# A transformer block's opening: modulation by slices of 128 channels, later vectors on GpSimd and ScalarE

## The chip, the cores and the metric

The kernel runs on one core of one Trainium2 chip. The metric is the device time of one execution in microseconds (us), lower is better. TensorE (PE) does matrix products, VectorE (DVE), ScalarE (ACT) and GpSimd (POOL) do elementwise work, and SyncE (SP) issues most DMA transfers. Each engine takes its instructions in one order that is fixed when the program is built, so an instruction that waits holds everything behind it on its engine.

## The reference

A block with two halves, each scaled and shifted by vectors made from a conditioning row `c`. S = 2048 positions, D = 512 channels, 32 heads of 16, window 256, F = 1792.

```python
mod = (_silu(c) @ w_mod).reshape(c.shape[0], 6, 1, -1)
sa, ca, ga, sb, cb, gb = (mod[:, 0], mod[:, 1], mod[:, 2], mod[:, 3], mod[:, 4], mod[:, 5])
h = _layernorm(x, axis=-1) * (1 + ca) + sa
x = x + ga * _A_ref(h, A_wqkv, A_wo)         # windowed attention
h = _layernorm(x, axis=-1) * (1 + cb) + sb
x = x + gb * _B_ref(h, B_w1, B_w3, B_w2)     # gated feed-forward
```

The six vectors of `mod` have 512 numbers each; the first two (`sa`, `ca`) are needed before the first product of the attention, the others much later.

## The kernel before

Activations stand with channels on the partitions: `hT` holds the normalised and modulated x, transposed, in four slices `k` of 128 channels. Every float32 operand of the large products is split in a high part in fp32r and the remainder, so each large product is three matmuls over 512 columns (high by high, high by low, low by high).

The program has a beginning and then units. The beginning works on four blocks `b` of 512 positions. Per block: four tiles `xt` of x are loaded (`load_x`); DVE takes mean and variance (`bn_stats`, `bn_aggr`); GpSimd raises the variance to -0.5 (`rstd_of`); DVE applies both (`ln_apply`, L456, four instructions); PE transposes 16 tiles of 128x128, four for each slice k (L737); ACT multiplies and adds the modulation (L463, from `modc`); DVE rounds to the high part (L465) and subtracts (L466). From `hT` PE then makes the values, 12 matmuls for each of 16 tiles (`values`, L759; ACT moves the result to `vS`, L763), and the queries and keys of units 0 to 2 (`unit_a`, 12 matmuls each, L548); the rows of these go by SP to `ringq` and `ringk` (L567, L569). The first two units' maximum scores (`unit_b`, L595 on PE, L604 on DVE) also lie in the beginning. The units proper start with L855.

`modulation(j, s, t0, at)` makes one vector of `mod`. Four chunks of `w_mod` (256 KB each) are loaded to a slot of `stage`, which is memory of `vS` that is not yet in use. PE multiplies them by silu(c) repeated 32 times (`row`, L678: four matmuls of 512 columns, each to 32 rows of the result), ACT copies the result (`out`, L684), PE adds the four parts and turns them to a column with products by a column of 1/32 (`turn`, L692, one output column each, or L689 for the two gate vectors, which stay rows), and DVE or ACT writes the result (`end`). Vectors 0 and 1 come first, 3, 4, 2 and 5 between the products of the values.

The order of the beginning is that of the numbers in the table `W`: each operation is put in a list with a time by `at(t, fn)`, and the list is sorted. The units have such a list of their own, from the table `X`, and a second schedule block; memory of the beginning (`p0`) is given back between the two (`pre.close()`).

Of the kernel before, what the change touches and what calls it, by code (L numbers as in the profile page):

```python
# [17 lines left out]
H, DH = 32, 16  # L18
# [31 lines left out]
W = dict(m=0.18, s=0.307, a=0.29, t=0.562, p=0.366, vs=1.748, vo=0.433, wq=(-1.444, 1.47, 1.587), wv0=-2.239, wvh=(-0.578, -0.445, -0.399, -0.345), wvl=(-0.193, -0.326, -0.374, -0.317), wp=1, A0=2.112, h0=0.452, h=6.002, hb=6.868, ls=3.035, la=0.875, rf=(-1.1, -0.393, 6.445), v=2, vt=1.562, mr=(-1.837, 1.507), mm=(3.653, 5.841, 7.356, 7.655), ml=(-1.346, 1.651, 2.536, 6.904), A=1.465, At=7.897, B=10.563)  # L50
# [3 lines left out]
XB = 6  # L54
# [238 lines left out]

ENGS = (
# [117 lines left out]
def block_kernel(ctx: ExitStack, tc: tile.TileContext, x, wqk, wv, wo, w13, w2, c, wmod, out):  # L412
# [9 lines left out]
    o32 = cst.tile([P, 32], F32, name="o32")  # L422
    nc.gpsimd.memset(o32, 1.0 / 32)
    modc = cst.tile([P, 4, KC], F32, name="modc")
    sc32 = cst.tile([P, KC, 32], F32, name="sc32")
# [15 lines left out]

    def rstd_of(pool, mv, n, tag):
        var = pool.tile([P, n], F32, name=tag + "v")
        nc.vector.tensor_scalar_add(var, mv[:, :n, 1], EPS)
        rs = pool.tile([P, n], F32, name=tag + "r")
        nc.gpsimd.tensor_tensor(out=rs, in0=var, in1=nhalf[:, :n], op=ALU.pow)
        return rs

    def ln_tile(pool, xin, mv, i):
        st = pool.tile([P, nc.vector.BN_STATS_DIM], F32, name="bst", bufs=4)  # L450
        nc.vector.bn_stats(st, xin)
        nc.vector.bn_aggr(mv[:, i], st)

    def ln_apply(pool, xin, mv, rs, i, tag):
        xn = pool.tile([P, D], F32, name=tag, bufs=4) if tag else xin
        nc.vector.tensor_scalar(xn, xin, mv[:, i, 0:1], rs[:, i:i + 1], op0=ALU.subtract,  # L456
                                op1=ALU.mult)
        return xn

    def mod_split(pool, hT, src, k, lo, at):  # L460

        h = pool.tile([P, BT], F32, name="h32", bufs=3)
        nc.scalar.activation(h, src, AF.Identity, bias=modc[:, at, k:k + 1],  # L463
                             scale=modc[:, at + 1, k:k + 1])
        nc.vector.tensor_copy(hT[:, 0, k, lo:lo + BT], h)  # L465
        nc.vector.tensor_tensor(out=hT[:, 1, k, lo:lo + BT], in0=h,  # L466
                                in1=hT.bitcast(F32)[:, 0, k, lo:lo + BT], op=ALU.subtract)

# [169 lines left out]

    xt = {}

    def load_x(t):
        xt[t] = p0.tile([P, D], F32, name="xt", bufs=XB)
        nc.sync.dma_start(xt[t], x[t * P:(t + 1) * P, :])


    stage = vS.rearrange("p t h d -> p (t h d)")[:, 4 * H * (DH + 1):12 * KC * P + 4 * H * (DH + 1)]
    stage = stage.rearrange("p (s k c) -> p s k c", s=3, k=KC)

    def load_mod(j, s, eng):
        for k in range(KC):  # L650
            eng.dma_start(stage[:, s, k], wmod[j, :, k])

    for t in range(2):
        load_x(t)
    load_mod(0, 2, nc.scalar)
    for t in range(2, 4):
        load_x(t)
    load_mod(1, 1, nc.sync)
    sc = cst.tile([P, KC], F32, name="sc")
    cst.tile([P, 24], F32, name="gap")  # L660
    nc.scalar.activation(sc, c_sb, AF.Silu)

    def fill_sc():
        nc.vector.tensor_copy(sc32, sc[:, :, None].to_broadcast([P, KC, 32]))

    def modulation(j, s, t0, at):

        v = {}

        def bank(n):  # L670
            v[n] = psA.tile([P, BT], F32, name="mx", bufs=MXB)
            return v[n]

        def row():

            ps = bank(0)
            for k in range(KC):
# [3 lines left out]
        def out():  # L681
            v["e"] = p0.tile([P, D], F32, name="h32", bufs=3)
            for n in range(2):
                nc.scalar.activation(v["e"][:, n * 256:n * 256 + 256], v[0][:, n * 256:n * 256 + 256], AF.Copy)  # L684

        def turn():
            ps = bank(1)
            if j in (2, 5):
                nc.tensor.matmul(ps[:32], o32, v["e"], start=True, stop=True)  # L689
                return  # L690
            for n in range(KC):
# [3 lines left out]
        def end():  # L695
            if j in (2, 5):
                r = p0.tile([P, D], F32, name="h32", bufs=3)
                nc.scalar.activation(r[:1], v[1][:1], AF.Copy)
                nc.sync.dma_start(g_dr[j // 5:j // 5 + 1, :], r[:1, :])
            else:  # L700
# [19 lines left out]
    def ln1(b, ts, ta, th, at):  # L720
        v = {}

        def stats(i):
            if i == 0:
                v["mv"] = p0.tile([P, 4, 2], F32, name="mv", bufs=2)
# [984 lines left out]
```

## Time and profile before

| | |
|---|---|
| time, median of 3 runs | 919.44 us (918.0 to 920.11) |
| the profiled execution: time | 918.07 us |
| its span, first to last instruction | 916.3 us |
| busy share of PE, DVE, POOL, ACT | 98%, 71%, 61%, 56% |

All positions in time below count from the start of the span of the profiled execution. "<-" in a row means that what stands left is written from what stands right; "[0.52 <-DVE modc L701]" means 0.52 us of idle time before the instruction, ended by that instruction of DVE. An instruction of PE has a duration with its way through the array in it; what a product costs in a row of products is the distance of the starts.

### The profile page before, as it was taken

To read this page: it belongs to the slowest core of one execution; us is meant where nothing else is said; L and a number is where in the kernel's file an instruction comes from. 1 tells how busy PE (TensorE), PEld (TensorE's weight loads), DVE (VectorE), ACT (ScalarE), POOL (GpSimd) and SP (SyncE) were. 2 spreads that over 40 slices of the span, in tenths; PEclk is the share of its full clock that TensorE was granted. 3 is DMA by queue.
4 is the path that set the end of the run, shared out by engine and by line. 5 is a ranking of instruction groups with operands and counts; after the bars stand their busy time and mean duration, and the time that the engine had idled before them with its cause. 6 is when DMAs were issued, how large, how long until landed. Compare 5 with 4: busy or idle time off the path is not lost.

```text
span 916.3 us, 18353 instructions
## 1 busy us (share of the span) xinstructions
PE 893.5 (98%) x6052; PEld 726.0 (79%) x6052; DVE 654.8 (71%) x1786; ACT 513.6 (56%) x962; POOL 555.2 (61%) x796
## 2 busy tenths in 40 slices
PE   6999999999999999989998999999999999999998
PEld 2688788888888888866776888888888888888886
DVE  7676778788887778786679668758568665565555
ACT  3433777778778777766597834343465334332330
POOL 6211687787888787867676356886569355435220
PEclk9999999999999999998999999999999999999999
DMA  9631456566655655567875677574272423231102
GB/s 330 201 93 36 109 158 171 165 173 171 178 161 165 174 159 156 144 170 220 266 224 184 211 245 247 174 235 145 85 264 65 159 76 104 66 100 43 46 24 93
DMA packets 126083, 141.73 MB, mean 155 GB/s; under 512 B 61090, under 2 KB 73890, under 8 KB 125988
## 3 DMA queue, kind: packets, MB, share of 16 engines
q1 hardware_dynamic: 125268, 139.51, 50.4%
q10 hardware_dynamic: 720, 1.05, 0.4%
q8 instruction: 48, 0.79, 0.4%
q14 instruction: 47, 0.39, 0.1%
HBM read 85.72 MB, written 34.61 MB: 131 GB/s over the span
## 4 chain that ended last, share of the span: by engine, by line
PE 85%; DMA 4%; DVE 4%; ACT 2%; POOL 2%; issue 2%; SPq 0%; ACTq 0%; POOLq 0%; DVEq 0%
PE st L1472 11%; PE mx L1472 10%; PE pj L548 9%; PE st L855 8%; PE po L905 8%; PE mx L595 7%; PE mx L1568 7%; PE st L1568 6%; PE st L759 5%; PE pj L1472 4%; PE po L1472 3%; PE po L1568 2%; PE pj L1568 2%; DMA vS<-in_wmod 1%; POOL pt L865 1%
## 5 line engine op out<-in xcount | busy, mean ns | idle before, releaser
L604 DVE CUSTOM_DVE_ANT_0 junk<-mx,mskq 128x320 bf16<-128x320 f32 (+4 forms) x512 | 216.5, 466 | 55.0 <-PE mx L595 53.0
L865 POOL TENSOR_SCALAR_AFFINE_SELECT pt<-pt 128x256 f32<-128x256 f32 x472 | 184.7, 413 | 65.9 <-ACT pt L892 26.4
L595 PE MATMUL mx<-ringk,ringq 96*128 96x320 f32 (+4 forms) x512 | 149.3, 314 | 1.6 <-DMA ringq<-qk 1.6
L548 PE MATMUL pj<-hT,wq 128*128 128x512 f32 x384 | 140.2, 401 | 0.0
L892 ACT ACTIVATE pt<-st 128x512 f32<-128x512 f32 (+1 forms) x216 | 117.3, 573 | 33.1 <-DVE st L882 27.6
L855 PE MATMUL st<-ringq,ringk 98*128 98x256 f32 (+1 forms) x536 | 128.4, 328 | 3.3 <-DMA ringq<-mT 1.9
L1067 POOL TENSOR_TENSOR w<-w,w 128x512 fp32r<-128x512 f32 (+2 forms) x49 | 85.2, 1754 | 55.9 <-ACT w L1066 55.2
L595 PEld LDWEIGHTS mx<-ringk,ringq 96*128 96x128 f32 x512 | 95.9, 190 | 13.5 <-issue 2.4
L855 PEld LDWEIGHTS st<-ringq,ringk 98*128 98x128 f32 x536 | 88.3, 191 | 13.3 <-issue 2.5
L905 PE MATMUL po<-pt,vS 128*17 128x128 f32 (+1 forms) x2144 | 89.0, 314 | 0.4 <-ACT pt L876 0.4
L548 PEld LDWEIGHTS pj<-hT,wq 128*128 128x128 f32 x384 | 71.6, 190 | 10.3
L905 PEld LDWEIGHTS po<-pt,vS 128*17 128x17 f32 x2144 | 60.8, 98 | 23.1 <-issue 5.1
L882 DVE COPY_PREDICATED st<-later,st 128x256 f32<-128x256 uint8 x152 | 62.0, 426 | 23.3 <-PE st L855 21.3
L1519 POOL TENSOR_TENSOR t<-t,t 128x512 f32<-128x512 f32 x25 | 33.5, 1342 | 65.4 <-DVE t L1507 65.4
L1472 PE MATMUL st<-b,w 128*128 128x512 f32 x270 | 67.0, 390 | 0.2 <-DVE x1a L1573 0.2
L1472 PEld LDWEIGHTS st<-b,w 128*128 128x128 f32 x270 | 50.5, 188 | 11.5 <-DVE x1a L1573 0.7
L876 ACT ACTIVATE pt<-pt 128x512 f32<-128x512 f32 (+1 forms) x96 | 52.6, 587 | 9.6 <-POOL pt L865 9.4
L860 ACT ACTIVATE pt<-st 128x512 f32<-128x512 f32 (+1 forms) x96 | 52.0, 546 | 8.8 <-PE st L855 8.1
L561 POOL TENSOR_TENSOR qk<-qkr,qk 128x512 fp32r<-128x512 f32 x32 | 41.5, 1298 | 20.0 <-ACT qk L557 19.8
L1066 ACT ACTIVATE w<-w 128x512 fp32r<-128x512 f32 (+2 forms) x56 | 42.4, 784 | 18.7 <-DMA w<-wraw 11.4
L1507 DVE TENSOR_TENSOR t<-mx,t 128x512 f32<-128x512 f32 x44 | 30.1, 685 | 29.4 <-ACT t L1514 12.5
L1507 DVE TENSOR_TENSOR t<-st,t 128x512 f32<-128x512 f32 x40 | 27.4, 686 | 26.7 <-ACT g L1495 9.3
(310 smaller groups left out, 1887.0 us busy)
## 6 DMA issues: line engine op xcount, KB each, us to landing
ringq<-qk SPq DMA_DIRECT2D x192, 64.0 KB, 2.1
ringk<-qk SPq DMA_DIRECT2D x96, 128.0 KB, 2.4
o_dr<-os SPq DMA_DIRECT2D x32, 256.0 KB, 2.2
w<-wsum SPq DMA_DIRECT2D x14, 512.0 KB, 4.3
w<-w2g SPq DMA_DIRECT2D x14, 512.0 KB, 3.7
jb<-in_w SPq DMA_DIRECT2D x24, 256.0 KB, 3.7
w<-wraw SPq DMA_DIRECT2D x14, 384.0 KB, 5.7
vS<-in_wmod SPq DMA_DIRECT2D x20, 256.0 KB, 5.0
```

The source lines that it names most:

```text
L548: nc.tensor.matmul(v["ps"], WQ[g][w][:, n // 3], hTp(i, n // 3, b * BT, BT), start=(n == 0), stop=(n == 3 * KC - 1))
L595: nc.tensor.matmul(v[i][:, :n], both_queries(a, gs), keys(NS, a, (gs + 1) * HP - n, n), start=True, stop=True)
L604: nc.vector.tensor_tensor_reduce(out=junk[:, :n], in0=v[i][:, :n], in1=mskq[:, WK - n:], scale=1.0, scalar=-3e38, op0=ALU.add, op1=ALU.max ...
L855: nc.tensor.matmul(piece(v[a, k], a, k, m), keys(NM, a, kb * P, P), queries(a, 4 * b + q, n), start=new, stop=not new or len(here(a, k)) = ...
L865: nc.gpsimd.affine_select(out=out, in_=in_, **w)
L882: nc.vector.copy_predicated(o, later, block(v[a, fk], a, fk, m))
L892: nc.scalar.activation(o, i, AF.Exp, scale=SCALE)
L905: nc.tensor.matmul(po[32 * i:32 * i + DH + 1, q * P:(q + n) * P], vS[:, 4 * b + j, 4 * g + i], piece(pt_of(a, k), a, k, m)[:, h], start=i ...
L1067: either(lambda e: e.tensor_tensor(out=lo(), in0=src(), in1=hi().bitcast(F32), op=ALU.subtract), 0.85, 0.06 + 0.0024 * n, key, kl + kh, kl ...
L1472: nc.tensor.matmul(ps(bk), WT[s, n][w][:, col], BB[t, k][r], start=start and c == 0, stop=stop and c == 5, skip_group_check=True)
L1507: return nc.vector.tensor_add(o, x, y)
L1568: nc.tensor.matmul(ps(bk), tiles[hk + (h,)][:, i * P:(i + 1) * P], w2_of(last, y, f), start=(m == 0), stop=(m == 5))
```

## The change

The two vectors needed first are made by slices of 128 channels: `mod_first(k, n)` loads the 512 KB of `w_mod` that make slice k of both vectors, and PE makes them with eight matmuls of one output column each, with the chunk of `w_mod` as the weights, so the result is a column at once; DVE adds (0, 1) and writes `modc` for slice k. The other four vectors are made without PE: `mod_later(i, n)` loads a row block of the transposed `w_mod` (256 KB, 16 of them through a ring of six slots), GpSimd multiplies it by silu(c) in every row, and ACT adds along the row with its accumulator. One transpose on PE turns the gate vectors to rows (`mod_end`). ACT loads `c` once more as a row for all 128 partitions (`crow`, 256 KB). `warm(i)` gives PE 24 products that nobody reads, from the identity in fp32r, the first 16 on half of the rows each. The order of the beginning is a list of 590 numbers (`ORDER0`); `BANK0` and `ENG0` say which PSUM pool and which of DVE and GpSimd an operation takes. Beginning and units are emitted in one schedule block.

```diff
-    def modulation(j, s, t0, at):
...
-        def row():
-
-            ps = bank(0)
-            for k in range(KC):
-                nc.tensor.matmul(ps[32 * k:32 * k + 32, :], sc32[:, k], stage[:, s, k], start=True,
-                                 stop=True)
...
-                nc.tensor.matmul(ps[:, n:n + 1], v["e"][:, n * P:(n + 1) * P], o32[:, 0:1],
-                                 start=True, stop=True)
...
+    sc_row = a1.tile([P, D], F32, name="qk2", bufs=1)
+    nc.scalar.dma_start(sc_row, crow.to_broadcast([P, D]))
+    sc = cst.tile([P, KC], F32, name="sc")
+    nc.scalar.activation(sc, c_sb, AF.Silu)
+    nc.scalar.activation(sc_row, sc_row, AF.Silu)
...
+    def mod_first(k, n):
+        if n == 0:
+            nc.sync.dma_start(raw_mod[:, k], wmod01[k])
+        elif n == 1:
+            v["mod", k] = bank(("mod", k), "mx")
+            for j in range(2):
+                for q in range(KC):
+                    nc.tensor.matmul(v["mod", k][:, j:j + 1], raw_mod[:, k, j, q], sc[:, q:q + 1],
+                                     start=(q == 0), stop=(q == KC - 1), skip_group_check=True)
+        else:
+            nc.vector.tensor_tensor(out=modc[:, 0:2, k], in0=v["mod", k][:, :2], in1=one, op=ALU.add)
...
+    def mod_later(i, n):
+        (m, k), s = divmod(i, KC), i % LATE
+        j = LATER[m]
+        if n == 0:
+            nc.sync.dma_start(ring[:, s], wmodT[m, k])
+        elif n == 1:
+            nc.gpsimd.tensor_tensor(out=ring[:, s], in0=ring[:, s], in1=sc_row, op=ALU.mult)
+        else:
+            to = gcol[:, i:i + 1] if m < 2 else modc[:, j - 1, k:k + 1]
+            nc.scalar.activation(ring[:, s], ring[:, s], AF.Copy, accum_out=to)
...
+    identr = a1.tile([P, BT], F32R, name="qk1", bufs=1)[:, :P]
+    nc.scalar.activation(identr, ident, AF.Copy)
+
+    def warm(i):
+        if i == 0:
+            v["warm"] = psA.tile([P, BT], F32, name="pj", bufs=1)
+        if i < 16:
+            n, rows, to = 2 if i >= 8 else 4, slice(HP * (i % 2), HP * (i % 2) + HP), po if i % 2 else v["warm"]
+        else:
+            n, rows, to = 4 if i < 20 else 1, slice(0, P), po
+        nc.tensor.matmul(to.rearrange("p (n c) -> p n c", n=4)[:, :n], identr[rows],
+                         identr[rows, None, :].to_broadcast([rows.stop - rows.start, n, P]), start=True, stop=True,
+                         skip_group_check=True)
...
     with tc.manual_schedule():
-        for fn in first + order:
+        for fn in begin + [units_open] + following(first) + order:
             fn()
```

Three places of the order. First PE from the first products of the program on. Before, from the last transposes of block 0 to the first products of the values (L737 transposes, L678 a modulation row, L759 and L548 products); the brackets name what an instruction waits for, with a lane of the DMA queues as DMAHW:

```order
L737 MATMUL st<-ident,xt 128x128 [waits Activation_49]
L737 MATMUL st<-ident,xt 128x128 x3
L678 MATMUL mx<-vS,sc_70 32x512 [waits DMAHW5_49,DVE_49]
L678 MATMUL mx<-vS,sc_70 32x512 [waits DMAHW6_49]
L678 MATMUL mx<-vS,sc_70 32x512 [waits DMAHW7_49]
L678 MATMUL mx<-vS,sc_70 32x512 [waits DMAHW0_49]
L759 MATMUL st<-wvh,hT 128x512 [waits DVE_49,Activation_49]
```

And of the changed kernel, first from the end of the throwaway products (L773) to the first transposes (L780), with two slices of the modulation (L709) between:

```order
L773 MATMUL po<-qk_138 128x512 x4
L773 MATMUL po<-qk_138 128x128 x4
L709 MATMUL st<-sc,vS 128x1 x16
L780 MATMUL st<-ident,xt_167 128x128
L780 MATMUL st<-ident,xt_180 128x128
```

Then, after the transposes of channel slices 0 and 1, from the third slice of the modulation to the fourth (L571 and L798 are products):

```order
L709 MATMUL mx<-sc,vS 128x1 x8
L780 MATMUL mx<-ident,xt_167 128x128
L780 MATMUL mx<-ident,xt_180 128x128
L780 MATMUL mx<-ident,xt_171 128x128
L780 MATMUL mx<-ident,xt_169 128x128
L571 MATMUL pj<-hT,wq_268 128x512
L798 MATMUL st<-wvh,hT 128x512 x3
L709 MATMUL mx<-sc,vS 128x1 x8
```

Before, all transposes of block 0 and a third modulation row stood ahead of the first product; now 24 throwaway products and two slices of the modulation stand ahead of the transposes, the third slice between those of channel slices 1 and 2, and four products ahead of the fourth, behind which come the transposes of channel slice 3.

Second DVE, around the four instructions that apply the normalisation of block 0. Before (L456 applies, L701 writes `modc`, L718 makes the low part of `wv`, L465 and L466 write `hT`):

```order
L444 TENSOR_SCALAR rs0v<-mv 128x4 [waits DVE_49]
L456 TENSOR_SCALAR xt<-xt,mv,rs0r 128x512 [waits Pool_49]
L456 TENSOR_SCALAR xt<-xt,mv,rs0r 128x512 x3
L701 TENSOR_SCALAR modc<-mx 128x4 [waits PE_49]
L718 TENSOR_TENSOR wvl<-vS,wvh 128x512 [waits DMAHW7_49,Activation_49]
L701 TENSOR_SCALAR modc<-mx 128x4 [waits PE_49]
```

Changed (L760 applies, L712 writes one slice of `modc`, L788 and L791 write `hT`, L560 the low part of the first query and key weights):

```order
L753 TENSOR_SCALAR va_195<-mv_182 128x4 [waits DVE_49]
L760 TENSOR_SCALAR xt_171<-xt_171,mv_182,rs_233 128x512 [waits Pool_49]
L712 TENSOR_TENSOR modc<-st,one 128x2 [waits PE_49]
L760 TENSOR_SCALAR xt_169<-xt_169,mv_182,rs_233 128x512
L760 TENSOR_SCALAR xt_167<-xt_167,mv_182,rs_233 128x512
L760 TENSOR_SCALAR xt_180<-xt_180,mv_182,rs_233 128x512
L712 TENSOR_TENSOR modc<-st,one 128x2 [waits PE_49]
L788 CAST hT<-h_266 128x512 [waits Activation_49]
L791 TENSOR_TENSOR hT<-h_266,hT 128x512 [waits DVE_49]
L560 TENSOR_TENSOR wq_274<-wqr,wq_268 128x512 [waits DMAHW2_49,Activation_49]
L712 TENSOR_TENSOR modc<-mx,one 128x2 [waits PE_49]
```

The write of the first slice, which waits for PE, now stands ahead of the second, third and fourth of the applying instructions. A few rows on, DVE stands like this, with the write of the fourth slice ahead of the low part of channel slice 1:

```order
L788 CAST hT<-h_270 128x512 [waits Activation_49]
L712 TENSOR_TENSOR modc<-mx,one 128x2 [waits PE_49]
L791 TENSOR_TENSOR hT<-h_270,hT 128x512 [waits DVE_49]
L788 CAST hT<-h_302 128x512 [waits Activation_49]
L791 TENSOR_TENSOR hT<-h_302,hT 128x512 [waits DVE_49]
L788 CAST hT<-h_304 128x512 [waits Activation_49]
L747 BN_STATS bst_313<-xt_205 128x6 [waits DMAHW5_49]
```

Third SP, where the rows of unit 0 are sent (L590, L592 to `ringk` and `ringq`). In the changed kernel loads for the later vectors (L720) stand between them, some of which wait for ACT to have read their slot:

```order
L592 DMA ringq<-qk_392 16x16x64 [waits DMAHW4_49,Activation_49]
L720 DMA vS<-in_wmodT 128x512 [waits DMAHW5_49,Activation_49]
L592 DMA ringq<-qk_392 16x16x64 [waits DMAHW6_49]
L590 DMA ringk<-qk_392 32x2x512 [waits DMAHW7_49]
L592 DMA ringq<-qk_392 16x16x64 [waits DMAHW0_49]
L592 DMA ringq<-qk_414 16x16x64 [waits DMAHW1_49,Pool_49]
L720 DMA vS<-in_wmodT 128x512 [waits DMAHW2_49,Activation_49]
```

Before, SP had there the loads of x of a later block and two stores of gate vectors among the same rows.

## Rows read from the trace of the kernel before

**Rows 1.** The page: busy time, share of the span and instructions of each engine.
```profile
PE 893.5 (98%) x6052; PEld 726.0 (79%) x6052; DVE 654.8 (71%) x1786; ACT 513.6 (56%) x962; POOL 555.2 (61%) x796
```

**Rows 2.** Busy by stage: us, PE, PEld, DVE, ACT, POOL, granted clock, DMA share, GB/s.
```profile
0.00:21.36 21.36, 12.67 (x57) 5.25 (x57) 16.15 (x26) 8.29 (x15) 14.21 (x27) 1.00 0.92 325
21.36:49.71 28.35, 28.35 (x144) 19.38 (x143) 17.02 (x33) 10.68 (x21) 6.41 (x6) 1.00 0.64 205
49.71:94.29 44.58, 44.58 (x222) 36.62 (x221) 30.71 (x102) 16.83 (x27) 6.34 (x5) 1.00 0.21 53
```

**Rows 3.** Timeline of the first 21.5 us: start, length, engine, line, operation, count.
```profile
1.23 2.55 ACTq L651 DMA_DIRECT2D vS<-in_wmod  x4
...
5.12 0.67 DVE L451 BATCH_NORM_STATS2 bst<-xt 128x6 f32<-128x512 f32 x1
...
10.16 1.03 POOL L446 TENSOR_TENSOR rs0r<-rs0v,nhalf 128x4 f32<-128x4 f32 x1 [3.06 <-DVE rs0v L444]
...
11.23 4.66 DVE L456 TENSOR_SCALAR xt<-xt,mv,rs0r 128x512 f32<-128x512 f32 x4 [1.15 <-POOL rs0r L446]
...
13.09 1.95 PE L692 MATMUL mx<-o,h 128*128 128x1 f32 x16
...
15.94 1.20 PE L737 MATMUL st<-ident,xt 128*128 128x128 f32 x9 [0.52 <-DVE modc L701]
...
18.82 0.41 DVE L465 CAST hT<-h 128x512 fp32r<-128x512 f32 x1
...
19.76 1.67 PE L678 MATMUL mx<-vS,sc 128*32 128x512 f32 x4 [0.30 <-DMA vS<-in_wmod]
...
21.36 0.50 PE L759 MATMUL st<-wvh,hT 128*128 128x512 f32 x1
```

**Rows 4.** Timeline of PE at the first and last modulation step among the products.
```profile
25.81 0.61 PE L759 MATMUL st<-wvh,hT 128*128 128x512 f32 x2
...
27.08 0.49 PE L759 MATMUL st<-wvl,hT 128*128 128x512 f32 x1
...
42.82 0.39 PE L759 MATMUL st<-wvh,hT 128*128 128x512 f32 x1
...
44.12 0.50 PE L759 MATMUL st<-wvl,hT 128*128 128x512 f32 x1
```

**Rows 5.** Line L678 in two stretches: durations in ns, least/median/most.
```profile
L678 PE MATMUL mx<-vS,sc x16: 592/1059/1062, 7.5 to 12.6; 128*32 128x512 f32 x16
...
L678 PE MATMUL mx<-vS,sc x8: 592/605/617, 18.1 to 20.8; 128*32 128x512 f32 x8
```

**Rows 6.** DMA: GB/s in 40 slices of 0 to 30 us; median us to landing.
```profile
GB/s 0 0 29 256 246 169 295 374 399 407 407 404 399 404 393 336 336 407 404 401 398 395 375 350 298 380 396 402 401 402 382 391 371 371 410 404 399 347 98 25
...
vS<-in_wmod ACTq DMA_DIRECT2D x4, 256.0 KB, 6.6
...
xt<-in_x SPq DMA_DIRECT2D x1, 256.0 KB, 2.9
```

**Rows 7.** Groups of POOL, ACT and DVE in the beginning: count, busy, mean ns.
```profile
L561 POOL TENSOR_TENSOR qk<-qkr,qk 128x512 fp32r<-128x512 f32 x5 | 6.8, 1367 | 19.8 <-ACT qk L557 19.8
...
L763 ACT ACTIVATE vS<-st 128x512 f32<-128x512 f32 x16 | 9.6, 597 | 24.6 <-PE st L759 24.6
...
L466 DVE TENSOR_TENSOR hT<-h,hT 128x512 fp32r<-128x512 f32 x16 | 11.1, 692 | 0.6
```

**Rows 8.** Timeline: a cast on DVE beside a busy POOL, another beside an idle one.
```profile
60.27 1.29 POOL L561 TENSOR_TENSOR qk<-qkr,qk 128x512 fp32r<-128x512 f32 x1 [1.07 <-ACT qk L557]
...
60.88 0.97 DVE L465 CAST hT<-h 128x512 fp32r<-128x512 f32 x1
...
62.49 0.42 DVE L465 CAST hT<-h 128x512 fp32r<-128x512 f32 x1
```

**Rows 9.** SP sends rows of unit 0: its timeline; the page, median to landing.
```profile
37.47 1.41 SPq L569 DMA_DIRECT2D ringq<-qk  x2
...
ringq<-qk SPq DMA_DIRECT2D x192, 64.0 KB, 2.1
```

More of the change, by code (lines that the diff above doesn't have):

```diff
@@ L411, in block_kernel @@
 @with_exitstack
-def block_kernel(ctx: ExitStack, tc: tile.TileContext, x, wqk, wv, wo, w13, w2, c, wmod, out):
+def block_kernel(ctx: ExitStack, tc: tile.TileContext, x, wqk, wv, wo, w13, w2, c, crow, wmod01, wmodT, out):
     nc = tc.nc
@@ L773, in block_kernel @@
+    ring = stage[:, stage.shape[1] - LATE * D:].rearrange("p (s c) -> p s c", s=LATE)
     ops = []
@@ new lines, in turn, with modulated, high @@
+    def turn(b, k):
+        v["t", b, k] = bank(("t", b, k), "mx")
+        for i in range(4):
+            nc.tensor.transpose(v["t", b, k][:, i * P:(i + 1) * P], xt[4 * b + i][:, k * P:(k + 1) * P], ident)
+    def modulated(b, k):
+        v["h", b, k] = p0.tile([P, BT], F32, name=f"h32{k % 2}")
+        nc.scalar.activation(v["h", b, k], v["t", b, k], AF.Identity, bias=modc[:, 0, k:k + 1],
+                             scale=modc[:, 1, k:k + 1])
+    def high(b, k):
+        nc.vector.tensor_copy(hT[:, 0, k, b * BT:b * BT + BT], v["h", b, k])
@@ new lines, in low, with value, value_out @@
+    def low(e, b, k):
+        e.tensor_tensor(out=hT[:, 1, k, b * BT:b * BT + BT], in0=v["h", b, k],
+                        in1=hT.bitcast(F32)[:, 0, k, b * BT:b * BT + BT], op=ALU.subtract)
+    def value(t, k, m):
+        if k == 0 and m == 0:
+            v["v", t] = bank(("v", t), "mx" if t == 3 else "st")
+        w, i = ((0, wvh), (0, wvl), (1, wvh))[m]
+        nc.tensor.matmul(v["v", t], hTp(w, k, t * P, P), i[:, k], start=(k + m == 0), stop=(k == KC - 1 and m == 2))
+    def value_out(t):
+        nc.scalar.activation(vS[:, t, :, :DH], v["v", t].rearrange("p (h d) -> p h d", d=DH), AF.Copy)
@@ L810, in block_kernel, with units_open @@
     for u in range(2):
-        unit_b(u, h0 + W["B"] + W["At"] * u, at, Y)
-    with tc.manual_schedule():
-        for _, _, fn, _ in sorted(ops, key=lambda o: o[:2]):
-            fn()
-    pre.close()
-    a2 = att.enter_context(tc.tile_pool(name="a2", bufs=1, reuse_waits="tile"))
+        unit_b(u, (30, 55)[u], at, y)
+    ops.sort(key=lambda o: o[:2])
+    begin = arranged([o[2] for o in ops], ops)
+    late = {}
+    def units_open():
+        pre.close()
+        late["a2"] = att.enter_context(tc.tile_pool(name="a2", bufs=1, reuse_waits="tile"))
@@ L949, in job_tile @@
     def job_tile(n):
-        jb[n] = a2.tile([P, D], F32, name=f"jb{n % 2}", bufs=1)
+        jb[n] = late["a2"].tile([P, D], F32, name=f"jb{n % 2}", bufs=1)
         return jb[n]
```

280 lines of the change are left out of this document (128 added, 152 removed), and 33 rows, old and new, of tables (BANK0, ORDER0).

## The prediction

> **What bounds the kernel now.** I read the page first. TensorE is busy for 98% of the span [rows 1], so time is won by taking work from TensorE, or where it stands still. By stage [rows 2], from the first product at 21.36 us to the first unit at 94.29 TensorE has work throughout (28.35 of 28.35 us, then 44.58 of 44.58), while VectorE has 47.7, ScalarE 27.5 and GpSimd 12.8 us of work in the same 72.9. Ahead of 21.36 TensorE works for only 12.67 us; there it waits for data. Behind 94.29 the order is the same in both kernels, and I let it take the same time.
>
> How it waits in the first stage is in the timeline [rows 3]: VectorE starts the statistics at 5.12, GpSimd gives the power at 11.19, VectorE needs 4.66 us to apply it, to 15.89, and the transposes go on behind that. The first product would have had its data at 19.23, when the first cast ended, but a modulation row stood ahead of it on TensorE, whose third chunk landed only for 19.76; so 21.36.
>
> **The sum, part by part.**
>
> *Modulation among the products, removed.* Seven pieces stand there: three rows (L678) and four turns (L692, L689). At 25.81 two products begin; at their distance of 0.23 us the next could start at 26.27, and it starts at 27.08: 0.81. The last piece: product at 42.82, next possible 43.05, in fact 44.12: 1.07. Read in this way the seven cost 0.81, 1.09, 0.81, 1.17, 1.20, 1.15 and 1.07 ([rows 4] has the first and the last of them); sum 7.3. Back comes one transpose for the gate vectors, 0.1.
>
> *The front.* ScalarE's queue carries 256 KB (`crow`) in place of 1 MB, so the x tiles land sooner: they and `crow` are 1.3 MB, which by the rates in slices of 0.75 us had been moved by 7.5 us [rows 6]. VectorE cannot start before about 5.1, since its instruction ahead is unchanged. Before, the four statistics with their aggregation and two waits for x lasted until GpSimd's start at 10.16; with earlier landings (0.67 and some 0.2 each, an estimate) they end by 9.2, and with a short step and GpSimd's 1.03 us the first applying instruction starts at 10.45, in place of 11.23 [rows 3]. It takes 4.66/4 = 1.17, to 11.6.
>
> There the new wait stands: VectorE's next instruction writes slice 0 of `modc` and holds the other three until TensorE has made that slice. TensorE makes it behind 24 throwaway products, and these wait for the identity that ScalarE copies behind silu of `crow`. `crow` is issued at 1.23; a transfer of 256 KB took 2.9 us for the first x tile and 6.6 in the median of the ScalarE queue, so it lands between 4.1 and 7.8 [rows 3, 6]; I take 5.2, since only 256 KB stand on that queue. ScalarE adds 0.6 and 0.3: the throwaways start near 6.2. They stream 8,704 columns; at 0.23 us for 512 that is 3.9 us. If the products on half of the rows run in pairs it is 2.5; no row shows such pairs. And the same modulation product took 1.059 us in the first stretch of work and 0.605 later [rows 5], 1.75 times, so 6.8 is the other end. I take 4.7, near the middle, to 10.9. The column that names the granted clock reads 1.00, which is 2.4 GHz, in both stretches [rows 2]; it does not show what the durations show.
>
> The Trainium skill ("TensorE: Matmul & The Clock Gate", "Part 1: The HAM clock gate") says that half rate is TensorE's default state and that activity releases it. By it the throwaways are paid in a pause and the products behind them are fast; the durations agree that the start is slow, and before the change the modulation rows had done that warming already.
>
> Eight matmuls of one column with their weights: sixteen passes took 1.95 us (L692) [rows 3]. So slice 0 is done at 12.85, its write at 13.1, against 11.6 where VectorE could have gone on: 1.5 us of hold. Applying ends at 16.9 (10.45 + 4.66 + two writes + 1.5), before at 15.89. Then TensorE in its new order: transposes of slices 0 and 1 (0.5 each, by the 0.12 us distance of the nine) to 17.95, modulation slice 2 to 19.9, transposes to 20.4, four products to 21.3, modulation slice 3 to 23.25, transposes to 23.75. Before, four products and all transposes were done at 21.36 + 4 x 0.23 = 22.3. The front loses **1.5 us**. With no hold it loses nothing (22.25); with `crow` at 7.8 and 6.8 us of throwaways the hold, and the loss, is 6.1.
>
> *The feed of block 0 and of block 1.* The fourth slice's write holds VectorE until 23.4, and ahead of the last low part it then has three low parts (0.69), two casts (0.42), four statistics (some 0.85 with their aggregation) and the low part of a `wv` chunk (0.69 like the others) [rows 7, 8]: 7.0 us, with the start of each some 7.5. TensorE has 33 products before it needs it, 7.5 us from 23.75; then eleven more until the transposes of block 1, which need one more power (1.03) and four applying instructions (0.5 each with GpSimd idle). That fits but for some tenths. With GpSimd busy it does not: a cast took 0.97 us beside a GpSimd instruction and 0.42 soon after [rows 8], and the four applying instructions of block 0, with GpSimd busy, 4.66. I take **1.0 us** of stall, bounds 0 and 4.
>
> The Trainium skill ("SBUF — State Buffer", "Who interferes with whom") says that VectorE's cast or two-operand work and GpSimd's work take turns at one pair of ports, each blocking the other for a whole instruction. The two casts agree. By that rule in full, with each of 24 casts and applying instructions of blocks 1 to 3 doubled, VectorE would get 0.55 x 24 = 13 us more; it has 25 us of idle time there, so this too would be a matter of single waits.
>
> *The later vectors.* Sixteen GpSimd multiplies at 1.37 us (nearest row: L561) are 21.9 us on an engine that idles for 60 of 72.9; sixteen ScalarE passes at 0.60 (L763) are 9.6 on one that idles for 45 [rows 2, 7]. Their results are needed only long after the first unit. GpSimd and ScalarE hide them: 0. If their place in line is wrong, they hold what stands behind: bounds 0 to 3, put with the rival below. On SP, unit 0's last query product ends near 31.5, ScalarE and GpSimd need 1.2 + 1.4, and nine rows with three loads between, at 0.7 us each, are out by about 41 and landed by 43 [rows 9]; TensorE comes to the first score at about 45, so the loads between cost nothing.
>
> *One block with the units:* no pause at 94.29 to be won; 0.
>
> Sum: -7.3 + 0.1 + 1.5 + 1.0 = **-4.7 us**: span 916.3 to 911.6, its time 918.07 to 913.4. The median of the runs shown lies 1.4 above that execution: **914.7 us**. The bounds give -7.8 to +3 and more.
>
> **The rivals.**
> *VectorE held by the first slice* for 4 to 6 us: `crow` lands late or the throwaways run one by one at the slow rate. For it: three engines in a row ahead of one wait. Against: TensorE has no other work there, and only 256 KB stand on that queue. The front loses 4.5 to 6: 917.7 to 919.2. The change would then do on the later vectors what it says and give it back in front.
> *The feed is what bounds*, so that the products only wait where modulation stood before: 3 to 5 us of stall in blocks 0 and 1 or behind slots of the ring: 916.7 to 919. Against: VectorE idled for 25 us there.
> *Slower: the slow rate in block 0.* Ahead of the products TensorE has only one-column matmuls, transposes and pauses for some 10 us. If the products then start at half rate, at 0.46 in place of 0.23 us, the gain is gone after 4.7/0.23 = 20 products, and after 29 of block 0's 60 the kernel is slower by over 0.2%; with all 60 it is 914.7 + 13.8 = 928. Against: before the change five microseconds of the same (one-column products, transposes, a pause of 0.5) lay between 13.09 and 18, and the modulation product at 18.1 ran in 0.605, not 1.059 [rows 3, 5].
>
> **Chances.** 0.2%, some 1.8 us, is about what a measurement of this kernel tells from no change. The forecast (911.5 to 917.5) 0.58; better than that (no hold, no stall) 0.05; VectorE held 0.15, half of it within 0.2%; the feed 0.12, two thirds of it faster; the slow rate, or a stall that I don't see, 0.10. Faster 0.58 + 0.05 + 0.07 + 0.08 = 0.78, of which I take off 0.05 for the runs' own spread of 2 us: 0.73; within 0.2% 0.15; slower 0.12. Range 910.5 to 920: it leaves out half of the best case and the slow rate.
>
> **What would show it.** First product at about 20.4 with four together and a second start at 23.8; the first score near 45 (49.71 before); the first unit's score at 89.6 (94.29). VectorE's second applying instruction starts about 1.5 us after the first ended, released by TensorE. Throwaways from 6.2 to 10.9. Sixteen L722 at about 1.4 us. The forecast fails if the first unit starts later than 92.5, and the way to it tells why: the hold in front, waits of TensorE for VectorE or GpSimd between 24 and 45, or products at a distance of 0.46.

## The result, and the profile after

The changed kernel takes 930.48 us (median of four runs: 928.0 to 930.6 in three, and 2255.8 in one that counts in no ratio), the kernel before 918.72 beside it: ratio 1.0118, interval 1.0091 to 1.0145. It is slower by 1.2%; 914.7 had been forecast. The profiled execution took 930.57 us, with a span of 928.8.

The page, busy time by engine; beside [rows 1]:
```profile
PE 903.7 (97%) x6057; PEld 736.3 (79%) x6057; DVE 658.5 (71%) x1780; ACT 519.1 (56%) x983; POOL 583.8 (63%) x819
```
Five more instructions on TensorE, and 10.2 us more of busy time. Busy time by stretch, columns as in [rows 2], with the boundaries where the same events fall now: up to steady products (the first product behind the last transposes of block 0; four products stand ahead of it), to the first score, to the first unit, and from the first product of the feed-forward part to the end:
```profile
0.00:27.09 27.09, 19.49 (x109) 17.95 (x109) 13.25 (x24) 5.69 (x9) 14.34 (x29) 0.81 0.59 214
27.09:47.25 20.16, 20.16 (x97) 16.26 (x96) 16.85 (x31) 11.59 (x24) 13.53 (x10) 1.00 0.69 202
47.25:98.01 50.76, 46.64 (x223) 36.81 (x222) 37.56 (x101) 22.81 (x51) 28.35 (x22) 1.00 0.32 94
...
489.70:928.80 439.10, 433.11 (x1881) 349.64 (x1879) 284.47 (x396) 183.38 (x295) 223.61 (x164) 1.00 0.41 133
```
And that last part in the kernel before, the same view:
```profile
485.90:916.30 430.40, 424.15 (x1881) 349.59 (x1879) 284.03 (x396) 183.01 (x296) 224.70 (x164) 1.00 0.42 135
```

| stretch | before, us | after, us | difference | forecast |
|---|---|---|---|---|
| start to steady products (before: 21.36 and four products) | 22.30 | 27.09 | +4.8 | +1.5 |
| to the first score (49.71; 47.25) | 27.41 | 20.16 | -7.25 | -7.3 + 0.1, with part of the 1.0 of the feed |
| to the first unit (94.29; 98.01) | 44.58 | 50.76 | +6.2 | rest of the 1.0 |
| to the feed-forward part | 391.6 | 391.7 | +0.1 | 0 |
| to the end | 430.4 | 439.1 | +8.7 | 0 |

So there are three losses, in three stages, against one gain of the size forecast. The largest stands where not one instruction was changed: the same 1,881 matmuls, at a granted clock of 1.00 in both, keep TensorE busy 433.11 us in place of 424.15, 4.8 ns more for each. By tiles (groups of that part from 560 to 900 us: count, busy us, mean ns), after:
```profile
L1527 PE MATMUL st<-b,w 128*128 128x512 f32 x222 | 55.3, 391 | 0.0
...
L1527 PE MATMUL mx<-b,wo 128*128 128x512 f32 x108 | 27.8, 395 | 0.0
```
The same groups before:
```profile
L1472 PE MATMUL st<-b,w 128*128 128x512 f32 x216 | 53.5, 390 | 0.0
...
L1472 PE MATMUL mx<-b,wo 128*128 128x512 f32 x108 | 27.1, 389 | 0.0
```
`b` and `w` both lie at the low end of SBUF; `wo`, like `o`, `wq` and `qk`, lies in the pools with `side="right"`, at the high end. Products with one operand from each end are the slow ones: their starts are some 233 ns apart there in place of 226.7, those of products with both operands at the low end 229. (SBUF is the memory on the chip; pools are set up from its low end, those with `side="right"` from its high end.) What the change does to the low end is to alter the small constants: `o32`, `sc32` and the unused tile `gap` go, `one` and `gcol` come. With sizes rounded up to 32 bytes they are 736 bytes now and were 1,408, so each later tile of the low end starts 672 bytes lower; the high end's stay.

The front, in the timeline (after):
```profile
6.72 0.63 ACT L665 ACTIVATE qk<-qk 128x512 f32<-128x512 f32 x1 [2.71 <-DMA qk<-in_crow]
...
7.60 0.79 PE L773 MATMUL pj<-qk 64*128 64x512 f32 x1 [7.60 <-ACT qk L764]
7.61 0.79 PE L773 MATMUL po<-qk 64*128 64x512 f32 x1
...
11.29 2.93 DVE L760 TENSOR_SCALAR xt<-xt,mv,rs 128x512 f32<-128x512 f32 x1 [1.14 <-POOL rs L756]
...
12.41 4.53 PE L709 MATMUL st<-sc,vS 128*128 128x1 f32 x32
...
14.34 0.16 DVE L712 TENSOR_TENSOR modc<-st,one 128x2 f32<-128x2 f32 x1
14.42 2.83 DVE L760 TENSOR_SCALAR xt<-xt,mv,rs 128x512 f32<-128x512 f32 x3
...
18.85 3.41 PE L709 MATMUL mx<-sc,vS 128*128 128x1 f32 x16
...
22.87 0.78 PE L571 MATMUL pj<-hT,wq 128*128 128x512 f32 x1
```
The throwaways (the 24 products that nobody reads) last from 7.60 to 12.4. VectorE is hardly held by the first slice: its first applying instruction takes 2.93 us beside GpSimd's memsets and ends at 14.22, and the slice is written at 14.34. What takes long is TensorE. Each float32 product of one column is two passes in the trace, so a slice has sixteen. The first sixteen start 112 ns apart, as before the change (1.95 us for sixteen, [rows 3]); in the second sixteen the distance goes from 112 to 213 ns; the next sixteen take 3.41 us, and the first four products start 0.43 to 0.58 us apart. Its granted clock (the number ahead of the last two of a row):
```profile
14.00:16.00 2.00, 2.00 (x16) 2.00 (x15) 1.87 (x4) 0.00 (x0) 1.92 (x2) 0.76 1.05 387
16.00:18.00 2.00, 2.00 (x9) 1.73 (x9) 1.32 (x3) 0.00 (x0) 0.51 (x1) 0.50 1.01 374
...
24.00:26.00 2.00, 2.00 (x13) 1.81 (x12) 0.00 (x0) 0.09 (x1) 0.00 (x0) 0.68 0.00 0
26.00:28.00 2.00, 2.00 (x16) 1.86 (x16) 1.10 (x4) 0.25 (x1) 0.00 (x0) 1.00 0.08 12
```
It falls from 2.4 to 1.2 GHz at 15.04 us, during one-column passes, and is back at 25.28; the trace of the kernel before has no such fall until 414.5.

The stage to the first unit: TensorE is busy 46.64 of 50.76 us, and where it stops it is released by VectorE. VectorE's groups there (count, busy, mean ns), and what stands beside them on GpSimd:
```profile
L760 DVE TENSOR_SCALAR xt<-xt,mv,rs 128x512 f32<-128x512 f32 x8 | 9.5, 1227 | 1.1 <-POOL rs L756 1.1
L788 DVE CAST hT<-h 128x512 fp32r<-128x512 f32 x9 | 6.1, 679 | 0.0
L791 DVE TENSOR_TENSOR hT<-h,hT 128x512 fp32r<-128x512 f32 x6 | 5.6, 935 | 0.1
```
```profile
71.21 5.56 POOL L722 TENSOR_TENSOR vS<-vS,qk 128x512 f32<-128x512 f32 x4
71.27 5.78 DVE L760 TENSOR_SCALAR xt<-xt,mv,rs 128x512 f32<-128x512 f32 x4 [1.12 <-POOL rs L756]
...
77.11 0.44 PE L780 MATMUL mx<-ident,xt 128*128 128x128 f32 x2 [1.07 <-DVE xt L760]
```
Four applying instructions run beside four of the later vectors' multiplies, some 1.5 us each (0.54 for the same four in the kernel before), and TensorE's transposes wait for them. The power that GpSimd raises isn't held back by its multiplies: in both kernels, and in e4 and e10 below, each power of blocks 1 to 3 starts within 0.1 us of VectorE's result for it.

### The profile page after: what moved, and what is told of

Its sections match the earlier page's. It is cut to its first block, busy times and chain, and to the rows that moved or that the text cites. A ratio compares the mean times of both kernels' runs of the same rounds, so it can differ in the third digit from the quotient of the medians.

```text
span 928.8 us, 18373 instructions
## 1 busy us (share of the span) xinstructions
PE 903.7 (97%) x6057; PEld 736.3 (79%) x6057; DVE 658.5 (71%) x1780; ACT 519.1 (56%) x983; POOL 583.8 (63%) x819
## 4 chain that ended last, share of the span: by engine, by line
PE 87%; DVE 6%; DMA 4%; SPq 1%; ACT 1%; issue 1%; POOL 1%; ACTq 0%; DVEq 0%; POOLq 0%
PE st L1527 11%; PE mx L1527 10%; PE pj L571 9%; PE st L910 9%; PE po L960 9%; PE mx L618 8%; PE mx L1623 7%; PE st L1623 6%; PE pj L1527 4%; PE po L1527 3%; PE po L1623 2%; PE st L798 2%; PE pj L1623 2%; DVE xt L760 1%; DVE b L1425 1%
## 5 line engine op out<-in xcount | busy, mean ns | idle before, releaser
L571 PE MATMUL pj<-hT,wq 128*128 128x512 f32 x384 | 139.0, 401 | 0.0
L571 PEld LDWEIGHTS pj<-hT,wq 128*128 128x128 f32 x384 | 71.7, 190 | 10.5 <-ACT vS L801 0.3
L1527 PEld LDWEIGHTS st<-b,w 128*128 128x128 f32 x270 | 50.5, 188 | 11.8 <-DVE x1a L1628 0.7
L1121 ACT ACTIVATE w<-w 128x512 fp32r<-128x512 f32 (+2 forms) x56 | 42.4, 784 | 18.1 <-DMA w<-wraw 12.0
```

The lines of the kernel that those rows point to most:

```text
L571: nc.tensor.matmul(v["ps"], WQ[g][w][:, n // 3], hTp(i, n // 3, b * BT, BT), start=(n == 0), stop=(n == 3 * KC - 1))
L1527: nc.tensor.matmul(ps(bk), WT[s, n][w][:, col], BB[t, k][r], start=start and c == 0, stop=stop and c == 5, skip_group_check=True)
```

## The experiments

Ratios are to the kernel before, timed on the same chip. "FF" stands for the part from the first feed-forward product to the end, with its row in the view by stretch as above.

### Feed-forward: where tiles start

**e1: 32 bytes more.**
```diff
     gcol = cst.tile([P, 2 * KC], F32, name="gcol")
+    cst.tile([P, 8], F32, name="pad")
```


> The changed kernel with 32 bytes per partition of unused tile behind gcol; not one instruction differs. In the kernel before every tile that is set up after the small constants begins at a multiple of 64 bytes, in the changed one at 32 beyond such a multiple; the pad puts it back on one. Theory A (addresses slow TensorE's products): the 512-column products of the feed-forward part come every 227 ns again instead of 231.7, the 8.8 us that the changed kernel loses from 515 us to the end come back, and the time is 921.7 us (919.5 to 923.5) beside 930.5. Rival (the slow products come from the state of the chip or from the order of the instructions): no change, 930.5 us and 231.7 ns.

930.71 us, ratio 1.0141 (1.0117 to 1.0165). Not repaired; FF:
```profile
491.06:928.50 437.44, 431.43 (x1881) 350.58 (x1879) 283.82 (x396) 183.49 (x295) 224.55 (x164) 1.00 0.40 133
```
A multiple of 64 isn't enough: busy time moves by only 1.7 us.

**e2: the kernel before without its unused tile.**
```diff
-    cst.tile([P, 24], F32, name="gap")
```


> The kernel before without its unused tile gap of 96 bytes; nothing else differs. Its later tiles then begin 32 bytes beyond a multiple of 64, as those of the changed kernel do. Theory A (addresses): products of the feed-forward part every 231.7 ns instead of 226.7 and a time of 927.5 us (925 to 930) beside 918.7. Rival (clock, order of instructions): 918.7 us and 226.7 ns as before.

928.83 us, ratio 1.012 (1.0096 to 1.0144). The kernel before loses as much as the change does, by the removal of a tile that nothing reads or writes, and loses it in FF (439.75 beside 430.40):
```profile
486.95:926.70 439.75, 433.48 (x1881) 350.31 (x1879) 282.80 (x396) 183.66 (x295) 223.76 (x164) 1.00 0.40 133
```
So addresses are the cause, but not by a step of 64.

**e5, e6, e11: other starts for the changed kernel.**
```diff
+    cst.tile([P, 40], F32, name="pad")                                   # e5
```
```diff
-            v["mv", b] = p0.tile([P, 4, 2], F32, name=f"mv{b % 2}")       # e6, and so for bst, va, rs
+            v["mv", b] = cst.tile([P, 4, 2], F32, name=f"mv{b % 2}")
+    cst.tile([P, 88], F32, name="pad")
```
```diff
-    c_sb = cst.tile([P, KC], F32, name="c_sb")                            # e11, and so for sc, one
+    c_sb = p0.tile([P, KC], F32, name="c_sb")
```


> The changed kernel with 160 bytes of unused tile behind gcol, so that the tiles set up after the small constants start 512 bytes lower than in the kernel before, instead of 672 (the changed kernel) or 640 (e1). In the traces so far the feed-forward products with both operands among these tiles come every 227.5 to 229 ns in the changed kernel and in e1, and those with one operand among the tiles of the other end of the memory, which did not move, every 232 to 234; in the kernel before all come every 226.7. Theory A2 (it matters how the starts of the two operands stand to each other, in steps of at most 512 bytes): both kinds come every 226.7 ns and the time is 921.5 us (919 to 924; the front's clock may move it). Rival (the step is 1024 or 2048 bytes): as e1, 231 ns and 930 us.

> The changed kernel with ten small tiles of the beginning set up among the constants and 352 bytes of unused tile, so that the later tiles start at the very addresses of the kernel before. Theory A2 and any other form of the address theory: products of the feed-forward part every 226.7 ns, 921.5 us (919 to 924). Rival (addresses have no part in it): 231 ns and 930 us.

> The changed kernel with three small constants set up with the tiles of the beginning, so that the later tiles start 768 bytes lower than in the kernel before: 256 bytes off a step of 512. If the step is 512 bytes, the feed-forward products come every 230 to 233 ns and the part from its first product to the end takes 436 to 440 us; if it is 256 or 128 bytes (e1 was 128 off, at 231.0), 226.7 ns and 430 us.

e5 925.41 us, ratio 1.0076 (1.0059 to 1.0092); e6 925.17, 1.0074 (1.0058 to 1.009); e11 929.25 in a single execution. FF of e5, then of e11:
```profile
494.50:924.70 430.20, 424.21 (x1881) 349.57 (x1879) 285.70 (x396) 182.92 (x295) 224.59 (x164) 1.00 0.41 135
```
```profile
497.40:927.50 430.10, 424.09 (x1881) 349.61 (x1879) 285.70 (x396) 182.83 (x296) 224.70 (x164) 1.00 0.41 136
```
All three have the feed-forward part of the kernel before (e6: 430.00 us, 423.94 busy); e5 and e6 missed their ranges because their front was slower (below). By the shift of the low end: 0, 512 and 768 bytes are fast, 96, 640 and 672 slow, that is 96, 128 and 160 bytes off a multiple of 256. A step of 256 bytes fits all six, 128 or 512 doesn't.

**e15: e2 with the high end moved by as much.**
```diff
+    rp = ctx.enter_context(tc.tile_pool(name="rp", bufs=1, side="right"))
+    rp.tile([P, 24], F32, name="gap")
     a1 = ctx.enter_context(tc.tile_pool(name="a1", bufs=1, side="right", reuse_waits="tile"))
```


> e2 (the kernel before without its unused tile) with an unused tile of 96 bytes at the other end of the memory too, so that the tiles of both ends start 96 bytes lower than in the kernel before. Theory A3 (it matters how the starts of a product's two operands stand to each other, in steps of 256 bytes): as in the kernel before, 424 us of busy time for the 1,881 matmuls from the first feed-forward product on, 430.4 us for the part, and 918.4 us. Rival (each tile for itself has to start at a multiple of 256 bytes, for instance for the transfers into it): as e2 or worse, 433 us of busy time and more, 928 us and more.

919.53 us, ratio 0.9999 (0.9987 to 1.0012):
```profile
487.70:918.00 430.30, 423.96 (x1881) 349.63 (x1879) 284.78 (x396) 183.30 (x295) 224.55 (x164) 1.00 0.42 135
```
With both ends moved by 96 bytes the products are fast again. So what counts is how the starts of the two operands stand to each other, modulo 256 bytes; it has to be as in the kernel before. Whether they are equal modulo 256 there, no run shows.

### The front

**e3: e1 without throwaways**, and **e8: e6 with them put among the one-column products.**
```diff
     def warm(i):                                                          # e3
...
-        nc.tensor.matmul(to.rearrange("p (n c) -> p n c", n=4)[:, :n], identr[rows],
...
+        return
```
```diff
+                    if q % 2:                                             # e8, in mod_first
+                        warm(20)
```


> e1 with the 24 throwaway products left out (they feed nothing). Theory: they hold TensorE's clock up until about 14 us and are in nobody's way, since the weights of the first slice's vectors land late; without them the vectors of slices 0 and 1 run at the lower clock, 3.4 us a slice instead of 2.3, and the products run steadily from about 29 us instead of 27.05: 1 to 3 us slower than e1. Rival (the throwaways hold TensorE up when the first slice has landed): the vectors start before 12.4 us and the time is that of e1 or up to 1.5 us less.

> e6 with the last eight throwaways taken from ahead of the one-column products and sixteen of 256 columns put among them, one behind every second. Theory (the clock falls because the one-column products leave TensorE nearly without columns): the granted clock stays at 1.00 from 12 to 28 us, products run steadily from about 25 us, and the time is 1 to 6 us below e6. Rival (so few columns don't hold it): the clock is at 0.50 in 16 to 24 us again, products run steadily from 27 us or later, and the time is that of e6 or up to 2 us more.

e3 931.16 us, ratio 1.0132 (1.0102 to 1.0162), the same as e1 within the spread of either: the rival. Its timeline (this execution took 926.50, the fastest of its four):
```profile
9.27 6.96 PE L710 MATMUL st<-sc,vS 128*128 128x1 f32 x32 [9.27 <-DMA vS<-in_wmod]
18.46 3.41 PE L710 MATMUL mx<-sc,vS 128*128 128x1 f32 x16
22.48 0.78 PE L571 MATMUL pj<-hT,wq 128*128 128x512 f32 x1
24.33 2.14 PE L710 MATMUL mx<-sc,vS 128*128 128x1 f32 x16
26.73 0.48 PE L571 MATMUL pj<-hT,wq 128*128 128x512 f32 x1
```
The first slice had landed at 9.27, 3.1 us before the throwaways end in the changed kernel. What the passes lose at the slow rate (6.96 us for 32 in place of 4.53) they win by starting earlier. e8 took 926.81 us, 1.0084 (1.0067 to 1.0101), no better than e6: the clock read 0.66 in 14 to 16 us and 0.50 from 16 to 34. The clock fell with these products in place too.

**e7: e6 with the first shift and scale as in the kernel before.** In the place of `mod_first`, on TensorE (a few operations ahead of block 0's products change places with it):
```diff
-                    nc.tensor.matmul(v["mod", k][:, j:j + 1], raw_mod[:, k, j, q], sc[:, q:q + 1],
+                nc.tensor.matmul(ps[32 * q:32 * q + 32, :], sc32[:, q], raw_mod[:, j, q], start=True, stop=True)
...
+                nc.tensor.matmul(v["mod", j][:, q:q + 1], v["e", j][:, q * P:(q + 1) * P], o32[:, 0:1], start=True,
+                                 stop=True)
```


> e6 with the first shift and scale made as in the kernel before (eight 512-column products of silu(c) repeated 32 times, then eight one-column sums), and without throwaways; the later vectors stay as the change makes them. Theory (the change loses its front to TensorE's 64 one-column products with their weight loads, which run partly at the lower clock): products run steadily from about 22.5 us instead of 27 to 33, and the time is 4 to 9 us below e6: 915.5 us (913 to 918), below the kernel before too. Rival (VectorE and GpSimd hold the front, not TensorE): steady products from 26 us or later, and a time within 2 us of e6.

920.47 us, ratio 1.003 (1.0015 to 1.0046). The first product behind the last transposes, here and in e6, and the stage from the first score to the first unit:
```profile
23.86 0.48 PE L570 MATMUL pj<-hT,wq 128*128 128x512 f32 x1
```
```profile
31.69 0.78 PE L571 MATMUL pj<-hT,wq 128*128 128x512 f32 x1
```
```profile
43.83:94.89 51.06, 47.73 (x223) 38.05 (x222) 36.42 (x101) 22.73 (x51) 28.38 (x22) 0.97 0.32 94
```
Steady products from 23.86 (31.69 in e6), the first score at 43.83, 9.1 us ahead of e6 and 5.9 of the kernel before: the theory of the front holds, though e7 doesn't part the number of passes from the clock that fell among them. Here too it falls, from 19.53 to 22.94. The total missed its range, since the next stage took 51.06 us again, 6.5 more than in [rows 2], and ate it all.

**e13, e14: the changed kernel and e6 once more**, nothing edited.

> The changed kernel once more, nothing edited. If what the front loses is drawn anew in each execution (by how long TensorE runs at its lower level), the steady products begin elsewhere than at 27.09 us, somewhere in 26.5 to 33.7 as in the runs with other addresses; if the layout of the memory sets it, they begin at 27.1 again and the first score comes at 47.2.

> e6 once more, nothing edited. If drawn anew: steady products somewhere in 26.5 to 33.7 us instead of at 33.1; if set by the layout: at 33.1 again, with the first score at 52.9.

e13 935.53 us, steady products from 29.07 (27.09 the first time), the first score at 51.26 (47.25); e14 923.31, from 28.92 (31.69), the first score at 49.92 (52.89). So the layout doesn't set it. That it changes from execution to execution on one chip is borne out by e3, whose four spread over 6.7 us where seven of the kernel before beside them spread over 1.9. e13's timeline of the same one-column passes, the first two slices fast, the third and fourth slow:
```profile
13.18 3.88 PE L709 MATMUL st<-sc,vS 128*128 128x1 f32 x32
...
19.19 3.41 PE L709 MATMUL mx<-sc,vS 128*128 128x1 f32 x16
...
25.06 3.41 PE L709 MATMUL mx<-sc,vS 128*128 128x1 f32 x16
...
29.07 0.78 PE L571 MATMUL pj<-hT,wq 128*128 128x512 f32 x1
```
Its granted clock was 0.50 from 16.5 to 33.6 us. Over the ten executions with these one-column passes (the changed kernel, e1, e3, e4, e5, e6, e8, e11, e13, e14) steady products began between 26.7 and 31.7 us and the first score came between 46.9 and 53.1; the changed kernel's first profile was one of the two luckiest.

### The stage before the first unit

**e4 and e10: e1 and e7 without GpSimd's multiplies.**
```diff
         elif n == 1:
-            nc.gpsimd.tensor_tensor(out=ring[:, s], in0=ring[:, s], in1=sc_row, op=ALU.mult)
+            return
```


> e1 without GpSimd's 16 multiplies of the later modulation rows (ScalarE sums the rows unmultiplied, so the two gates and the second shift and scale are not those of the reference). Theory (VectorE's operations are stretched while GpSimd multiplies, and TensorE waits for VectorE): the normalisation of a tile on VectorE falls from a mean of 1119 ns to below 950, the stage from the first score to the first unit falls from 50.8 us to 46 to 48, and the time is 3 to 5 us below e1. Rival (VectorE has too much of its own work, whatever GpSimd does): the stage stays within 1 us, and so does the time.

> e7 without GpSimd's 16 multiplies of the later rows (ScalarE sums the rows unmultiplied, so the two gates and the second shift and scale are not those of the reference). In e7 the first score comes at 43.83 us, 5.9 before that of the kernel before, and the first unit at 94.89, 0.6 after it: the stage between takes 51.07 us as in every run with the multiplies (48.97 to 51.50), beside 45.78 in e4 without them. Theory (GpSimd's multiplies stretch VectorE's operations, and TensorE waits for those): stage of 45 to 46.5 us, first unit near 89.5, time 915.0 us (913 to 917). Rival (the early scores only wait for later blocks, whatever GpSimd does): stage of 50 us or more, time 919.5 to 921.

e4 927.56 us, 1.0103 (1.0087 to 1.012); e10 915.61, 0.9974 (0.9962 to 0.9987). The stage, in e1, e4 and e10:
```profile
51.09:100.06 48.97, 46.33 (x223) 36.90 (x222) 35.69 (x101) 22.84 (x51) 28.26 (x22) 1.00 0.33 98
```
```profile
49.92:95.70 45.78, 45.53 (x224) 36.92 (x222) 31.24 (x98) 22.74 (x51) 11.45 (x10) 1.00 0.36 105
```
```profile
45.08:90.58 45.50, 45.25 (x224) 36.91 (x222) 31.27 (x98) 22.74 (x51) 11.44 (x10) 1.00 0.39 110
```
TensorE hardly waits any more, and VectorE does nearly the same instructions in 31.3 us in place of 36 to 38. In e4 the applying and the subtracting ones went to means of 700 and 713 ns (1227 and 935 in the changed kernel), while the casts stayed (666, 679):
```profile
L761 DVE TENSOR_SCALAR xt<-xt,mv,rs 128x512 f32<-128x512 f32 x8 | 5.3, 700 | 1.1 <-POOL rs L757 1.1
```
The multiplies cost this stage 3.2 us (e4 beside e1, on which it is built) and 5.6 (e10 beside e7, where 3.4 us of the stage also ran at the lower clock). Counted to the first unit it is 4.4 (100.06 to 95.70) and 4.3 us (94.89 to 90.58).

**e9: multiply and sum in one instruction on VectorE**, and **e12: the multiplies 10 us earlier.**
```diff
-            nc.gpsimd.tensor_tensor(out=ring[:, s], in0=ring[:, s], in1=sc_row, op=ALU.mult)
+            nc.vector.tensor_tensor_reduce(out=ring[:, s], in0=ring[:, s], in1=sc_row, scale=1.0, scalar=0.0,
+                                           op0=ALU.mult, op1=ALU.add, accum_out=to)
```
```diff
-    ring = stage[:, stage.shape[1] - LATE * D:].rearrange("p (s c) -> p s c", s=LATE)      # e12, with an order of its own
+    ring = [stage[:, BT * n:BT * n + BT] for n in (0, 1, 2, 3, 4, 5, 6, 7, 8, 9, 10, 11, 5, 6, 7, 8)]
```


> e7 with each later row multiplied and summed by one instruction on VectorE, in place of a multiply on GpSimd and a sum on ScalarE. Theory: VectorE is busy 43.8 of the 60 us from 30 to 90 in e4, without multiplies; sixteen times some 0.75 us (by the 692 ns of a subtraction of 512 columns and the 81 ns of reading a sum) make 12 us more, which still fits, so the stage falls to 46 to 48.5 us and the time to 916.5 us (914.5 to 919). Rival (the added work stands in VectorE's queue ahead of what TensorE waits for, up to five of them in a row, and costs what the contention did): stage of 50 us or more, 919.5 to 922.5 us.

> e7 with the later rows loaded earlier (eight at once behind the second block's inputs, into the staging place of the first shift and scale, which is free from about 16 us; then four, then four) and multiplied by GpSimd about 10 us earlier, eight of the sixteen before 40 us, where TensorE has products in stock and doesn't wait for VectorE. Theory (what the multiplies cost depends on whether TensorE waits for VectorE where they stand): the stage from the first score to the first unit falls from 51.07 us to 47 to 49.5 and the time to 917.5 us (915.5 to 920). Rival (VectorE only falls behind earlier): stage of 50.5 us or more, 920 to 923 us.

e9 929.12 us, 1.0122 (1.0101 to 1.0144): the rival, and worse than it said. The stage took 57.98 us, TensorE busy 49.40 of them; up to five of the new instructions stand in a row ahead of what TensorE waits for. The granted clock read 0.91 over it, so part of the loss is the lower clock. e12 (here the loads of the last four rows go out at 42.4 us to places whose rows are summed from 45.1 us on, so some of the later vectors aren't the reference's) 922.98, 1.0058 (1.0044 to 1.0071), with a stage of 50.5 us: the rival too. The applying instructions of the second block, 1.92 us for four in e7, now stand beside the multiplies, and TensorE waits there:
```profile
33.31 4.80 DVE L744 TENSOR_SCALAR xt<-xt,mv,rs 128x512 f32<-128x512 f32 x4 [1.13 <-POOL rs L740]
...
38.17 0.44 PE L759 MATMUL mx<-ident,xt 128*128 128x128 f32 x2 [1.53 <-DVE xt L744]
```
GpSimd also waited 4.59 us for rows that e12 loads late, so e12 says nothing of the best order.

No version of the change that computes the reference beat the kernel before; e7 comes nearest, at 1.003.

## Why the prediction was wrong, point by point

- **Modulation among the products, removed, -7.3:** right. With steady products from start to end the stretch to the first score fell by 7.25 us.
- **Throwaways from 6.2 to 10.9:** length right (4.8 us; 4.7) by luck, start late by 1.4, since `crow` was there at 6.72 only. The products on half of the rows did start in pairs, 0.01 us apart, and at the slow rate, so two errors cancelled. That they pay for themselves was wrong: e3 does without them in the same time.
- **The front loses 1.5 us because slice 0 holds VectorE:** the step that failed in mechanism. The x tiles didn't land sooner: applying began at 11.29, forecast at 10.45, before at 11.23. VectorE was then held by the slice for 0.12 us only; GpSimd's memsets stretched its first applying instruction instead, so that applying ended at 17.2, near the forecast 16.9, by luck. What the sum had wrong is the rate behind that. I had taken 1.95 us a slice [rows 3] and 0.23 us a product throughout; the first slice kept to that, and then TensorE's clock fell: slice 2 took 3.41 and the first four products 1.86 in place of 0.9, so that the transposes of slice 3 ended 3.3 us late. The loss was 4.8 us, and in other executions with these passes the first score came up to 5.8 us later still. Without these passes (e7) it is gone.
- **The feed of blocks 0 and 1, 1.0 us between 24 and 45:** TensorE didn't wait there (busy 20.16 of 20.16 us to the first score). The waits came behind it, 4.1 us of them.
- **The rival of the slow rate** was right in kind and wrong in place: it struck the front's one-column passes and the first few products, not block 0 as a whole (in e13 the products went on at 0.43 us until 33.6). The argument against it, that TensorE had come through such a stretch before the change, didn't carry over.
- **The later vectors are hidden, 0:** failed. GpSimd had the time, but its multiplies slow VectorE, on which TensorE then waits: 6.2 us in the stage, 3.2 to 5.6 of them shown by e4 and e10. What makes up the rest of the 6.2 stays open. I had seen the casts [rows 8], and had held VectorE's 25 us of idle time against them; the waits fall on single chains (statistics, power, applying, transposes) that have no such reserve. The Trainium skill ("SBUF — State Buffer", "Who interferes with whom"), which has the two engines take turns, spoke against the change here. The four applying instructions beside the four multiplies agree, at 1.5 us each. I worked out 13 us of added VectorE time by it; the row has 6.9 (37.56 beside 30.71).
- **Behind 94.29 all takes the same time:** failed by 8.7 us, the largest share, and no rival had it. The order is indeed the same; the addresses aren't (e2, e5, e6, e15). That they cost nothing was taken without a reason.

## What to carry to other kernels

A change of a small constant moves every tile behind it: keep the starts of a product's two operands to each other as they were, modulo 256 bytes, across both ends of the memory, and read the mean duration of untouched products after any change. Idle time of an engine is no cover for work that slows another engine on a chain to TensorE: price the chain, not the share. A one-column pass with weights of 128 by 128 took 112 ns at the higher clock and 213 at the lower, about half of a product with 512 columns, and the clock fell among them; wide products and a turn were quicker here.

## What the runs showed of the hardware that I had not expected

- 512-column products took 395 ns in place of 389 (mean, clock 1.00) when the starts of their two operands had moved to each other by other than a multiple of 256 bytes; over the 1,881 matmuls that is 2.1% more busy time. Why the memory does so isn't shown, nor that 256 is the step for other shapes.
- One program had its first score at 47.3 or 51.3 us, by how long TensorE stayed at the lower level (15.0 to 25.3, 16.5 to 33.6 us). What decides that is open: it fell with e8's wide products among the narrow ones too.
- The view of the granted clock reads 1.00 ahead of the first change that the trace recorded, whatever the level: in e3 and e6 it read so while sixteen passes took 3.41 us. Their first records are a rise at 24.96 and at 34.42 us; in e3 passes went from 213 to 112 ns apart just there. So the throwaways ran at the lower level too: the changed kernel's first record is a rise at 11.62. The 1.00 of [rows 2] for the start means as little: the first record of the kernel before is a rise at 11.72.
- VectorE's fused multiply and sum of 512 columns took 0.69 us in most cases of e9, in a row one each 0.61 us; the mean of the sixteen was 0.87.
